# An mLSTM cell and a gated feed-forward block on one core: constant products in TensorE's pauses, late gates first, both sums of the first group at once, and weight blocks converted two columns ahead

## The chip, the cores and the metric

The kernel runs on one core of one Trainium2 chip. The metric is the device time in microseconds (us), from start to end of one execution; for the kernel before it is the median of three runs.

## The reference

Two blocks follow each other. The first is an mLSTM cell for 4 batches x 8 heads, 768 steps and a head dimension of 40. For each batch and head it keeps a matrix state and runs

```python
m_new  = maximum(f + m, i)
f_stab, i_stab = exp(f + m - m_new), exp(i - m_new)
C = f_stab * C + i_stab * outer(v_t, k_t)
n = f_stab * n + i_stab * k_t
y_t = sigmoid(o_t) * (C @ q_t) / maximum(abs(n . q_t), 1)
```

The heads of a step are then joined to a row of 320 numbers, 3072 rows in all, and the second block is `out = (silu(x @ w_gate) * (x @ w_val)) @ w_out` with 1536 hidden columns. The activations are 32-bit floats. The three weight matrices are 64-bit floats.

## The kernel before

**Groups.** The 768 steps are cut into six groups of 128 steps (L, `NG` = 6), and each group into two halves of 64 (SUB). One group of all batches makes 512 rows of x (`TW`). For each group the kernel does the cell, then the hidden layer, then the projection. The cell of group n is woven into the hidden layer of group n-1; only the cell of group 0 stands alone at the start.

**The cell of a group** is worked in two parts P (16 of the 32 batch-heads each). `turn` transposes k and q on TensorE (L292) and copies them out of PSUM. `scores` multiplies them (L307), `weigh` (L314) multiplies by the weights `w_sb`, which come from the gates. `weigh_values` (L317) scales v; `add` (L329) makes the sums of outer products of a half, for one half or for both (`parts`); `next_state` (L339 to L343) decays the old state with `dec` and adds the sum. A ring of three states `C_ring` is kept. `attend` (L351, L356) multiplies the queries by the states and the weights by v. `gather` (L366 to L377) adds both and forms the denominator, `gate` (L382) multiplies by the sigmoid of o, `divide` (L387, L389) writes x, and `seam` (L402) transposes x into `xT`.

**The gates.** The weights need running sums and running maxima of the gates. Those of group 0 (`f0`, `i0`, L258 to L265) are done first, spread over 128 partitions. The ten later halves lie in `f_sb`, `i_sb` (32 partitions x 640): `late_sums` (L270 to L274), `late_maxima` (L277 to L282, which also stores the maxima to DRAM as `M_dram`) and `late_turns` (L501 to L516: ten transposes, then the decays `dec` through one matmul). These three are run after the first, second and third hidden column of group 0. For the groups from 1 on, `weights_load` (L410) loads the maxima back in a spread form, `weights_sub` (L414), `weights_mask` (L419) and `weights_exp` (L423) make `w_sb` of them, and `sig` (L426) is the sigmoid of o.

**The hidden layer** (`hidden`, L527 to L531) does one column block m of 128 at a time, twelve in a group: ten matmuls of 512 columns for gate and value together, a SiLU on ScalarE, a product on VectorE into `h_sb`. **The projection** of group 0 (`project_all`, L548) holds four sums of 320 columns in PSUM and goes through m; the later groups' (`project`, L541) go one batch after the other. `result` (L535, L536) copies the sums out of PSUM on ScalarE and stores them.

**The weights.** A 64-bit float is taken as two 32-bit words and turned into a 32-bit float on the engines, block by block (18 blocks j: twelve hidden columns, six of w_out): `scale` on ScalarE (L180, L181; the low words are scaled in place), `join` on VectorE (L189, L190), `rounded` on GpSimd or VectorE (L197). `convert` is the three in a row. Ten loads (`piece_load`) bring the words; two use memory that is needed only later (`h_sb`, `wo_sb`), the others a pool `raw` of two buffers.

**Order.** The order of instructions on each engine is the order of the calls; nothing is moved by a scheduler. Each engine works through its list in order. `slots[m]` lists what is issued after the hidden column m of group 0, and `after[m]` what follows step m of its projection; a second `slots` does it for the later groups. In the kernel before, block m + 2 is converted after column m has been issued, its activation and product included. PSUM has two rings of four banks: "gen" for the hidden layer and the projection, "cell" for all the rest. A new tile in a ring waits for the reader of the tile four before it. Nearly all loads go through the queue of SyncE in program order.

`burn` (L432) issues matmuls of a tile of zeros whose result nobody reads; seven of them start the kernel.

Of the kernel before, what the change touches and what calls it, by code (L numbers as in the profile page):

```python
# [9 lines left out]
F32 = mybir.dt.float32  # L10
# [14 lines left out]
def kernel(  # L25
# [46 lines left out]
    def flat(t):  # L72
        return t.rearrange("p c t -> p (c t)")
# [45 lines left out]
    def gate_rows(a):  # L119
        return a.rearrange("b h s -> (b h) s")  # L120

    def spread_rows(a):
        return gate_rows(a)[:, 0:L].unsqueeze(0).to_broadcast([128 // BH, BH, L])

    nc.scalar.dma_start(out=flat(f0), in_=spread_rows(f_gate))
    nc.sync.dma_start(out=flat(i0), in_=spread_rows(i_gate))

# [47 lines left out]
    def scale(j):  # L175
        if j in blocks:
            lo, hi, dst = blocks[j]
            a, d = hi.shape[1], hi.shape[2]
            top = conv.tile([128, NKC * 128], F32, name="top", bufs=2).rearrange("p (a d) -> p a d", a=a)
            nc.scalar.mul(top, hi.bitcast(F32), 2.0 ** -112)  # L180
            nc.scalar.mul(lo.bitcast(I32), lo, 2.0 ** -29)  # L181
            blocks[j] = (lo, top.bitcast(U32), dst)
# [11 lines left out]
    def rounded(j, eng=None):  # L194
        if j in blocks:
            lo, both, dst = blocks.pop(j)
            (eng or nc.gpsimd).tensor_tensor(dst.bitcast(I32), both.bitcast(I32), lo.bitcast(I32), op=ALU.add)  # L197
# [10 lines left out]
    piece_load(0)  # L208
    load(o_sb, o_gate, 0, 0)
    load(o_sb, o_gate, 0, 1)  # L210
    nc.sync.dma_start(out=flat(f_sb), in_=gate_rows(f_gate)[:, L:])
    nc.sync.dma_start(out=flat(i_sb), in_=gate_rows(i_gate)[:, L:])
# [71 lines left out]
    M_dram = tc.dram_tile([BH, S - L], F32, name="M_dram")  # L284

# [37 lines left out]
    def add(P, parts=(0, 1)):  # L323
        ps = {i: small("add") for i in parts}
        order = QUAD if len(parts) == 2 else ((parts[0], 0), (parts[0], 1))
        for a in range(UA):
            for i, two in order:
                h = P * UH + 2 * a + two
                nc.tensor.matmul(ps[i][half(two), a, :], lhsT=k_sb[half(i), h, :], rhs=vw_sb[half(i), h, :],  # L329
                                 start=True, stop=True)  # L330
        return ps
# [4 lines left out]
    def next_state(s, P, ps):  # L336
        a = slice(P * UA, (P + 1) * UA)
        if s == 0:
            nc.scalar.copy(state(1)[:, a], ps)  # L339
            return  # L340
        nc.gpsimd.tensor_tensor(state(s + 1)[:, a], state(s)[:, a],  # L341
                                dec[:, s - 1, a].unsqueeze(2).to_broadcast([128, UA, D1]), op=ALU.mult)
        nc.vector.tensor_tensor(state(s + 1)[:, a], state(s + 1)[:, a], ps, op=ALU.add)  # L343
# [115 lines left out]
    A, V, G = nc.scalar, nc.vector, nc.gpsimd  # L459
    first_weights(0)  # L460
    turn(0, (V, V), (A, A))
    first_weights(1)
    tpe = bank("tp_e")[:, 0:BH]
    nc.tensor.transpose(tpe, flat(e0[0:BH]), idb)
    nc.vector.tensor_copy(e_T[:, 0], tpe)
    weigh_values(G, 0)
    sp = scores(0)
    weigh(0, sp)
    ps = add(0, (0,))
    next_state(0, 0, ps[0])  # L470
    turn_one(1, k_sb, kT, (A, A))
    at = attend(0, 0)
    y0, den0 = gather(0, 0, *at)
    turn_one(1, q_sb, qT, (A, V))
    weigh_values(G, 1)
    sp = scores(1)
    weigh(1, sp)
    ps = add(1, (0,))
    next_state(0, 1, ps[0])
    scale(0)  # L480
    join(0)
    at = attend(0, 1)
    sig(0)
    sig(1)
    gate(0, y0, G)
    divide(0, den0, G)
    rounded(0)
    y1, den1 = gather(0, 1, *at)
    seam(0, 0, (A, A, A, A))
    gate(1, y1, V)  # L490
    divide(1, den1)
    seam(0, 1, (A, V, A, V))
    scale(1)
    join(1)
    rounded(1, V)

    def late_turns():
        for src, dst in ((i_sb, g_T), (step1, e_T)):
            tp = bank("tp_g")[:, 0:NG * BH].rearrange("p (c h) -> p c h", h=BH)
            for c in range(1, NG):  # L500
                nc.tensor.transpose(tp[:, c, :], flat(src[:, 2 * c - 2:2 * c]), idb)  # L501
            nc.vector.tensor_copy(dst[:, 1:, :], tp[:, 1:, :])
        pair = early.tile([BH, PP], F32)
        nc.vector.reduce_sum(pair, idb.rearrange("p (a two) -> p a two", two=2), axis=AX.X)
        half_s = early.tile([BH, 2], F32)
        nc.vector.reduce_sum(half_s, idb.rearrange("p (a two) -> p two a", two=2), axis=AX.X)
        halves = early.tile([BH, 2, DP], F32)
        nc.vector.tensor_copy(halves, half_s.unsqueeze(2).to_broadcast([BH, 2, DP]))
        dec_r = early.tile([BH, NS - 1, PP], F32)
        for e, c0, n in ((e0[0:BH, 1:], 0, 1), (step1, 1, NS - 2)):  # L510
            nc.vector.tensor_tensor(dec_r[:, c0:c0 + n], pair.unsqueeze(1).to_broadcast([BH, n, PP]),
                                    e[:, :, last].to_broadcast([BH, n, PP]), op=ALU.mult)
        dps = bank("dec_ps")[:, 0:(NS - 1) * PP]
        nc.tensor.matmul(dps, lhsT=halves.rearrange("p a b -> p (a b)"), rhs=dec_r.rearrange("p c a -> p (c a)"),
                         start=True, stop=True)
        nc.vector.tensor_copy(dec.rearrange("p c a -> p (c a)"), dps)  # L516


# [3 lines left out]
    def hidden(g, m):  # L522
        ps = [bank("gv_ps", "gen") for _ in range(2)]
        x = xT(g)
        for kc in range(NKC):
            for i in range(2):
                nc.tensor.matmul(ps[i], lhsT=wgv_sb[half(i), PAIRS[kc][i], ts(m, 128)], rhs=x[half(i), kc, :],  # L527
                                 start=(kc == 0), stop=(kc == NKC - 1))
        sg = work.tile([128, TW], F32, name="sg")
        nc.scalar.activation(sg, ps[0], AF.Silu)  # L530
        nc.vector.tensor_tensor(hid(g, m), sg, ps[1], op=ALU.mult)  # L531
# [32 lines left out]
    def do_add(parts=(0, 1)):  # L564
        for P in range(2):
            live["add", P] = add(P, parts)

    def do_state(s, P):
        for i, ps in live.pop(("add", P)).items():
            next_state(s + i, P, ps)  # L570
# [15 lines left out]
    def first_state():  # L586
        do_add((1,))
        for P in range(2):
            do_state(0, P)

    def load_all(dst, a, n):
        for P in range(2):
# [4 lines left out]

    slots = {
        0: [run(convert, 2), run(late_sums)],
        1: [run(convert, 3), run(late_maxima), run(piece_load, 4), run(piece_load, 5)],  # L600
        2: [run(convert, 4), run(late_turns)],
        3: [run(convert, 5), run(first_state), run(load_all, k_sb, k, 1), run(load_all, q_sb, q, 1),
            run(weights_load, 1), run(load_all, v_sb, v, 1)],
        4: [run(convert, 6)],
        5: [run(convert, 7), run(piece_load, 6)],
        6: [run(convert, 8), run(turn, 0, (A, A), (A, V))],
        7: [run(convert, 9), run(turn, 1, (A, A), (A, V)), run(weights_sub, 1, 0), run(weights_mask, 0),
            run(piece_load, 7)],
        8: [run(convert, 10), run(weights_sub, 1, 1), run(weights_mask, 1), run(load_all, o_sb, o_gate, 1)],
        9: [run(convert, 11), run(piece_load, 8), run(weights_exp, 0), run(weights_exp, 1),  # L610
            run(weigh_values, G, 0), run(weigh_values, G, 1), run(do_scores), run(do_weigh, 0)],
        10: [run(convert, 12), run(do_weigh, 1), run(do_add), run(do_state, 2, 0), run(do_state, 2, 1)],
        11: [run(convert, 13), run(piece_load, 9), run(do_attend, 1, 0), run(do_gather, 1, 0, False)],
    }
    for m in range(NFC):
        hidden(0, m)
        for f in slots[m]:
            f()
    after = {
        0: [run(do_attend, 1, 1), run(convert, 14)],  # L620
        1: [run(do_gather, 1, 1, False), run(sig, 0), run(sig, 1), run(do_gate, 0), run(do_gate, 1),
            run(load_all, k_sb, k, 2), run(load_all, q_sb, q, 2), run(load_all, v_sb, v, 2), run(weights_load, 2)],
        2: [run(convert, 15)],
        3: [run(do_divide, 0), run(do_divide, 1), run(load_all, o_sb, o_gate, 2)],
        4: [run(convert, 16)],
        5: [run(seam, 1, 0, (A, V, A, V)), run(seam, 1, 1, (A, V, A, V))],
        6: [run(convert, 17)],
        7: [run(weights_sub, 2, 0), run(weights_mask, 0)],
        8: [run(weights_sub, 2, 1), run(weights_mask, 1)],
        9: [run(weights_exp, 0), run(weights_exp, 1)],  # L630
        10: [run(sig, 0), run(sig, 1), run(weigh_values, G, 0)],
        11: [run(weigh_values, G, 1)],
    }
    project_all(0, after)
    early_scope.close()
# [4 lines left out]
    for g in range(1, NG):  # L640
        n, f = g + 1, g + 2
        slots = {m: [] for m in range(NFC)}
        if n < NG:
# [9 lines left out]
            slots[10] = [run(do_divide, 1)]  # L653
            slots[11] = [run(seam, n, 0, (A, V, A, V)), run(seam, n, 1, (A, V, A, V))]
# [51 lines left out]
```

## Time and profile before

| what | us |
|---|---|
| time, median of 3 runs (616.28 to 620.67) | 618.82 |
| span of the profiled execution | 614.9 |
| TensorE busy | 578.1 (94%) |
| VectorE busy | 210.7 (34%) |
| ScalarE busy | 150.8 (25%) |
| GpSimd busy | 111.5 (18%) |
| mean granted TensorE clock | 0.955 |
| first hidden matmul of group 0 starts | 37.84 |
| projection of group 0 starts, ends | 127.91, 159.03 |
| hidden layer of group 1 starts | 166.64 |

Times count from the start of the span. PE is TensorE, PEld its weight loads, DVE is VectorE, ACT is ScalarE and POOL is GpSimd. L527 is line 527 of the listing above. In a line of the timeline stand the start, the time it took, the engine and line, what was written from what, and the number of instructions; in brackets stand the idle time of the engine just before and what ended it. One line can stand for several instructions of a kind. In a table by stage each engine has its busy time and (x) its number of instructions; then come the granted clock of TensorE (1.00 is full), the busy share of the DMA engines and what they moved in GB/s. The chain of work goes back from the last instruction to what released each; its lines have a start, a time and the work.

From 166 us on, each of the groups 1 to 4 takes 91.3 us (the projections of the groups begin at 233.97, 325.31, 416.64 and 507.96 us in the chain), and TensorE is nearly always busy there. Ahead of it lie the cell of group 0, the hidden layer of group 0 with the cell of group 1 and most of the conversion of the weights, and the projection of group 0.

### The profile page before, as it was taken

To read this page: it belongs to the slowest core of one execution; us is meant where nothing else is said; L and a number is where in the kernel's file an instruction comes from. 1 tells how busy PE (TensorE), PEld (TensorE's weight loads), DVE (VectorE), ACT (ScalarE), POOL (GpSimd) and SP (SyncE) were. 2 spreads that over 40 slices of the span, in tenths; PEclk is the share of its full clock that TensorE was granted. 3 is DMA by queue.
4 is the path that set the end of the run, shared out by engine and by line. 5 is a ranking of instruction groups with operands and counts; after the bars stand their busy time and mean duration, and the time that the engine had idled before them with its cause. 6 is when DMAs were issued, how large, how long until landed. Compare 5 with 4: busy or idle time off the path is not lost.

```text
span 614.9 us, 13142 instructions
## 1 busy us (share of the span) xinstructions
PE 578.1 (94%) x5880; PEld 342.6 (56%) x5880; DVE 210.7 (34%) x371; ACT 150.8 (25%) x240; POOL 111.5 (18%) x109
## 2 busy tenths in 40 slices
PE   8868699799599999999999999999999999999997
PEld 5733345466385556655556655557655557644465
DVE  4457446575123452023452023452023550011100
ACT  3434346351431011521011521111521111011100
POOL 2133135733500213200213200113200110000000
PEclk9659699799899999999999999999999999999999
DMA  9881799359330443030562020451000000000000
GB/s 125 160 168 31 151 167 229 99 120 164 67 66 1 67 90 55 22 54 2 67 103 42 33 44 6 62 111 34 33 1 4 1 3 16 28 0 1 0 12 32
DMA packets 129920, 37.92 MB, mean 62 GB/s; under 512 B 120424, under 2 KB 125032, under 8 KB 129864
## 3 DMA queue, kind: packets, MB, share of 16 engines
q1 hardware_dynamic: 129732, 37.02, 33.6%
q8 instruction: 46, 0.75, 0.6%
q14 instruction: 10, 0.08, 0.1%
q10 hardware_dynamic: 132, 0.07, 0.0%
HBM read 33.06 MB, written 4.01 MB: 60 GB/s over the span
## 4 chain that ended last, share of the span: by engine, by line
PE 72%; ACT 1%; POOL 0%; issue 0%; ACTq 0%
PE gv_ps L527 43%; PE o_ps L541 21%; PE inter L351 1%; PE sp L307 1%; PE add L329 1%; PE tp_kq L292 1%; PE intra L356 1%; PE tp_x L402 1%; ACT sg L530 0%; POOL w_sb L419 0%; ACT xT L115 0%; ACT o_sb L426 0%; ACT L426 0%; ACT w_sb L423 0%; ACT z_sb L535 0%
## 5 line engine op out<-in xcount | busy, mean ns | idle before, releaser
L527 PE MATMUL gv_ps<-xT,wgv_sb 64*128 64x512 f32 x1440 | 328.9, 606 | 11.5 <-ACT z_sb L535 7.6
L527 PEld LDWEIGHTS gv_ps<-xT,wgv_sb 64*128 64x128 f32 x1440 | 146.4, 191 | 168.8 <-issue 149.9
L531 DVE TENSOR_TENSOR h_sb<-sg,gv_ps 128x512 f32<-128x512 f32 x72 | 49.4, 687 | 325.9 <-ACT sg L530 287.8
L541 PE MATMUL o_ps<-wo_sb,h_sb 128*128 128x320 f32 x480 | 130.5, 433 | 0.0
L530 ACT ACTIVATE sg<-gv_ps 128x512 f32<-128x512 f32 x72 | 43.0, 597 | 298.1 <-PE gv_ps L527 298.1
L541 PEld LDWEIGHTS o_ps<-wo_sb,h_sb 128*128 128x128 f32 x480 | 90.8, 190 | 38.2 <-issue 0.8
L341 POOL TENSOR_TENSOR C<-C,dec 128x328 f32<-128x328 f32 x22 | 15.9, 734 | 172.5 <-DVE C L343 172.5
L535 ACT COPY z_sb<-o_ps 128x320 f32<-128x320 f32 x24 | 10.1, 424 | 106.3 <-PE o_ps L541 104.4
L419 POOL TENSOR_SCALAR_AFFINE_SELECT w_sb<-w_sb 64x1024 f32<-64x1024 f32 x20 | 26.0, 1302 | 26.8 <-DVE w_sb L414 25.9
L548 PE MATMUL o_ps<-wo_sb,h_sb 128*128 128x320 f32 x96 | 26.6, 436 | 0.0
L382 POOL TENSOR_TENSOR o_sb<-o_sb,y_sb 128x640 f32<-128x640 f32 x11 | 15.7, 1428 | 58.3 <-DVE y_sb L373 48.4
L317 POOL TENSOR_TENSOR vw_sb<-v_sb,w_sb 128x656 f32<-128x656 f32 x12 | 15.4, 1301 | 40.7 <-issue 26.6
L373 DVE TENSOR_TENSOR y_sb<-y_sb,intra 64x328 f32<-64x328 f32 x44 | 21.7, 493 | 2.5 <-PE intra L356 1.6
L548 PEld LDWEIGHTS o_ps<-wo_sb,h_sb 128*128 128x128 f32 x96 | 18.0, 190 | 7.3
L329 PEld LDWEIGHTS add<-vw_sb,k_sb 64*64 64x64 f32 x768 | 17.2, 152 | 8.7 <-issue 4.1
L329 PE MATMUL add<-vw_sb,k_sb 64*64 64x41 f32 x768 | 18.4, 244 | 3.8 <-DVE w_sb L314 3.8
L402 PE MATMUL tp_x<-ident,x_sb 64*128 64x64 f32 x240 | 14.2, 245 | 5.9 <-ACT xT L115 3.2
L351 PEld LDWEIGHTS inter<-C,qT 64*64 64x64 f32 x768 | 14.2, 149 | 7.9 <-issue 6.8
L314 DVE TENSOR_TENSOR w_sb<-sp,w_sb 128x512 f32<-128x512 f32 x24 | 15.4, 683 | 8.0 <-PE sp L307 5.0
L402 PEld LDWEIGHTS tp_x<-ident,x_sb 64*128 64x128 f32 x240 | 11.5, 150 | 11.0 <-ACT xT L115 4.4
L307 PE MATMUL sp<-qT,kT 64*64 64x64 f32 x768 | 14.3, 223 | 3.0 <-ACT qT L115 1.4
L307 PEld LDWEIGHTS sp<-qT,kT 64*64 64x64 f32 x768 | 12.7, 137 | 7.6 <-issue 4.3
(111 smaller groups left out, 371.4 us busy)
## 6 DMA issues: line engine op xcount, KB each, us to landing
w_sb<-M_dram SPq DMA_DIRECT2D x10, 512.0 KB, 7.4
k_sb<-in_k_dram SPq DMA_DIRECT2D x12, 320.0 KB, 6.0
q_sb<-in_q_dram SPq DMA_DIRECT2D x12, 320.0 KB, 6.3
v_sb<-in_v_dram SPq DMA_DIRECT2D x12, 320.0 KB, 6.5
o_sb<-in_o_gate_dram SPq DMA_DIRECT2D x12, 320.0 KB, 6.9
raw<-in_moe_w_out_dram SPq DMA_DIRECT2D x3, 1280.0 KB, 5.9
out_dram<-z_sb SPq DMA_DIRECT2D x24, 160.0 KB, 1.8
raw<-in_moe_w_gate_dram SPq DMA_DIRECT2D x3, 640.0 KB, 8.5
```

Source lines behind the costliest of these rows:

```text
L307: nc.tensor.matmul(sp[two][half(i), a, :], lhsT=kT[half(two), P * UA + a, half(i)], rhs=qT[half(two), P * UA + a, half(i)], start=True, st ...
L329: nc.tensor.matmul(ps[i][half(two), a, :], lhsT=k_sb[half(i), h, :], rhs=vw_sb[half(i), h, :], start=True, stop=True)
L341: nc.gpsimd.tensor_tensor(state(s + 1)[:, a], state(s)[:, a], dec[:, s - 1, a].unsqueeze(2).to_broadcast([128, UA, D1]), op=ALU.mult)
L351: nc.tensor.matmul(inter[two][half(i), a, :], lhsT=qT[half(two), P * UA + a, half(i)], rhs=state(2 * n + i)[half(two), P * UA + a, :], sta ...
L373: nc.vector.tensor_tensor(t, t, intra[i][half(c)], op=ALU.add)
L402: nc.tensor.transpose(tp[i][:, c - cs[0], b, :], x_sb[half(i), 2 * P + b, ds(PAIRS[c][0] * HP, 2 * HP)], ident[half(i), half(i)])
L419: nc.gpsimd.affine_select(w, w, compare_op=ALU.is_ge, fill=NEG, base=0, pattern=[[0, UH], [1, SUB]], channel_multiplier=-1)
L527: nc.tensor.matmul(ps[i], lhsT=wgv_sb[half(i), PAIRS[kc][i], ts(m, 128)], rhs=x[half(i), kc, :], start=(kc == 0), stop=(kc == NKC - 1))
L530: nc.scalar.activation(sg, ps[0], AF.Silu)
L531: nc.vector.tensor_tensor(hid(g, m), sg, ps[1], op=ALU.mult)
L541: nc.tensor.matmul(p, lhsT=hid(g, m)[:, ts(u, L)], rhs=wo_sb[:, m, :], start=(m == 0), stop=(m == NFC - 1))
L548: nc.tensor.matmul(ps[u], lhsT=hid(g, m)[:, ts(u, L)], rhs=wo_sb[:, m, :], start=(m == 0), stop=(m == NFC - 1))
```

## The change

It has five parts, all in how the work is ordered; the arithmetic stays, but for one sum that is formed another way.

1. **Constant products.** `burn` is called six more times, in places of the start where TensorE waits for other engines: 3, 2, 4, 3, 4 and 8 matmuls, 24 in all. They are to keep TensorE's clock up. Each call takes a bank of the "cell" ring.
2. **Late gates first.** `f_sb` and `i_sb` are loaded at the beginning, through ScalarE's queue; `late_sums` is issued at the start, right after group 0's gates; `late_maxima` moves from the second hidden column to the first. The decays are split: `decay_rows` after the second column, the transposes after the third, the matmul after the fourth. The first weights of columns (`piece_load(0)`) come after o.
3. **Both sums of the first group at once.** `first_sums` forms the sums of both halves in the start and copies them to states 1 and 2; `second_state` later adds the decayed state 1 to state 2 (two operations on GpSimd). The separate second sums after the fourth column go.
4. **Two columns ahead.** The conversion of block m + 2 is issued inside `hidden(0, m)`, ahead of its activation and product. The scaled low words get a tile of their own (`low`), and `top` and `low` have one buffer each, where `top` had two. The blocks 9, 10 and 11 are rounded on VectorE.
5. **Order elsewhere.** gate and divide of group 0 go to VectorE, and the first `weigh_values` too. The slots of the cell of group 1 move by up to a column; exponentials, sigmoids and `weigh_values` of group 2 follow the projection of group 0 and its output copies, instead of standing ahead of them; in the later groups `seam(n, 0)` moves from slot 11 to slot 10.

```diff
+    nc.scalar.dma_start(out=flat(f_sb), in_=gate_rows(f_gate)[:, L:])
+    nc.scalar.dma_start(out=flat(i_sb), in_=gate_rows(i_gate)[:, L:])
...
-            top = conv.tile([128, NKC * 128], F32, name="top", bufs=2).rearrange("p (a d) -> p a d", a=a)
+            top = conv.tile([128, NKC * 128], F32, name="top", bufs=1).rearrange("p (a d) -> p a d", a=a)
             nc.scalar.mul(top, hi.bitcast(F32), 2.0 ** -112)
-            nc.scalar.mul(lo.bitcast(I32), lo, 2.0 ** -29)
+            low = conv.tile([128, NKC * 128], I32, name="low", bufs=1).rearrange("p (a d) -> p a d", a=a)
+            nc.scalar.mul(low, lo, 2.0 ** -29)
...
-    piece_load(0)
     load(o_sb, o_gate, 0, 0)
     load(o_sb, o_gate, 0, 1)
-    nc.sync.dma_start(out=flat(f_sb), in_=gate_rows(f_gate)[:, L:])
-    nc.sync.dma_start(out=flat(i_sb), in_=gate_rows(i_gate)[:, L:])
+    piece_load(0)
     piece_load(1)
...
     M_dram = tc.dram_tile([BH, S - L], F32, name="M_dram")
+    late_sums()
...
+    def first_sums(P):
+        ps = add(P)
+        for i in range(2):
+            nc.scalar.copy(state(i + 1)[:, P * UA:(P + 1) * UA], ps[i])
+
     first_weights(0)
     turn(0, (V, V), (A, A))
     first_weights(1)
+    burn(3)
+    weigh_values(V, 0)
+    sp = scores(0)
+    weigh(0, sp)
+    first_sums(0)
+    turn_one(1, k_sb, kT, (A, A))
     tpe = bank("tp_e")[:, 0:BH]
...
-    weigh_values(G, 0)
-    sp = scores(0)
-    weigh(0, sp)
-    ps = add(0, (0,))
-    next_state(0, 0, ps[0])
-    turn_one(1, k_sb, kT, (A, A))
+    burn(2)
     at = attend(0, 0)
+    weigh_values(G, 1)
     y0, den0 = gather(0, 0, *at)
     turn_one(1, q_sb, qT, (A, V))
-    weigh_values(G, 1)
+    burn(4)
+    sig(0)
+    sig(1)
     sp = scores(1)
     weigh(1, sp)
-    ps = add(1, (0,))
-    next_state(0, 1, ps[0])
+    first_sums(1)
+    burn(3)
+    gate(0, y0, V)
+    divide(0, den0)
+    at = attend(0, 1)
+    y1, den1 = gather(0, 1, *at)
     scale(0)
-    join(0)
-    at = attend(0, 1)
-    sig(0)
-    sig(1)
-    gate(0, y0, G)
-    divide(0, den0, G)
-    rounded(0)
-    y1, den1 = gather(0, 1, *at)
+    burn(4)
     seam(0, 0, (A, A, A, A))
+    burn(8)
     gate(1, y1, V)
     divide(1, den1)
+    join(0)
+    rounded(0, V)
+    scale(1)
     seam(0, 1, (A, V, A, V))
-    scale(1)
     join(1)
-    rounded(1, V)
+    rounded(1)
...
+    def second_state():
+        old = work.tile([128, PP, D1], F32, name="y_sb")
+        nc.gpsimd.tensor_tensor(old, state(1), dec[:, 0].unsqueeze(2).to_broadcast([128, PP, D1]), op=ALU.mult)
+        nc.gpsimd.tensor_tensor(state(2), state(2), old, op=ALU.add)
...
-    def hidden(g, m):
+    def hidden(g, m, first=()):
...
+        for f in first:
+            f()
         sg = work.tile([128, TW], F32, name="sg")
...
+    on_vector = (9, 10, 11)
     slots = {
...
+        0: [run(load_all, k_sb, k, 1), run(load_all, q_sb, q, 1), run(piece_load, 5), run(late_maxima)],
+        1: [run(decay_rows)],
+        2: [run(late_turns), run(weights_load, 1)],
+        3: [run(decay)],
+        4: [run(second_state), run(piece_load, 6), run(load_all, v_sb, v, 1)],
+        5: [run(turn, 0, (A, A), (A, V))],
+        6: [run(turn, 1, (A, A), (A, V)), run(piece_load, 7)],
+        7: [run(weights_sub, 1, 0), run(weights_mask, 0)],
+        8: [run(weights_sub, 1, 1), run(weights_mask, 1), run(weights_exp, 0), run(weights_exp, 1),
+            run(weigh_values, G, 0), run(weigh_values, G, 1), run(piece_load, 8)],
+        9: [run(do_scores), run(do_weigh, 0), run(load_all, o_sb, o_gate, 1)],
+        10: [run(do_weigh, 1), run(do_add), run(do_state, 2, 0), run(do_state, 2, 1), run(piece_load, 9)],
+        11: [run(do_attend, 1, 0), run(do_gather, 1, 0, False)],
     }
+    piece_load(4)
     for m in range(NFC):
-        hidden(0, m)
+        hidden(0, m, [run(convert, m + 2, V if m + 2 in on_vector else None)])
...
     project_all(0, after)
+    weights_exp(0)
+    weights_exp(1)
+    sig(0)
+    sig(1)
+    weigh_values(G, 0)
+    weigh_values(G, 1)
...
-            slots[10] = [run(do_divide, 1)]
-            slots[11] = [run(seam, n, 0, (A, V, A, V)), run(seam, n, 1, (A, V, A, V))]
+            slots[10] = [run(do_divide, 1), run(seam, n, 0, (A, V, A, V))]
+            slots[11] = [run(seam, n, 1, (A, V, A, V))]
```

## The prediction

> **What bounds the kernel now.** TensorE, but not evenly. I read the page's slices first, then the table by stage, then TensorE's timeline with its idle times, last the chain of work.
>
> ```profile
> PE   8868699799599999999999999999999999999997
> PEclk9659699799899999999999999999999999999999
> ```
>
> Each slice is 15.4 us. From the twelfth on TensorE is busy at full clock; the loss lies in the first eleven.
>
> ```profile
> core 0: us, PE busy (x) PEld busy (x) DVE busy (x) ACT busy (x) POOL busy (x), PEclk, DMA share, GB/s
> 0.00:37.80 37.80, 29.21 (x708) 22.60 (x708) 19.82 (x48) 15.35 (x30) 10.93 (x20) 0.72 0.96 155
> 37.80:58.30 20.50, 18.49 (x61) 7.26 (x62) 11.47 (x16) 7.78 (x10) 4.99 (x3) 0.77 0.28 54
> 58.30:67.90 9.60, 1.94 (x12) 1.33 (x12) 5.83 (x13) 3.95 (x5) 2.42 (x2) 0.64 0.92 188
> 104.50:127.90 23.40, 18.56 (x426) 11.91 (x424) 13.01 (x19) 10.64 (x14) 13.21 (x11) 0.85 0.40 98
> 127.90:166.60 38.70, 30.58 (x269) 21.68 (x264) 20.73 (x37) 16.11 (x23) 20.28 (x16) 0.96 0.79 130
> ```
>
> No stage is full on any other engine. The clock column shows a second loss: a slower TensorE in the first 68 us.
>
> ```profile
> 37.84 2.04 PE L527 MATMUL gv_ps<-xT,wgv_sb 64*128 64x512 f32 x2 [0.69 <-ACT xT L115]
> 41.28 11.87 PE L527 MATMUL gv_ps<-xT,wgv_sb 64*128 64x512 f32 x38 [1.40 <-DVE wgv_sb L197]
> 60.93 0.67 PE L501 MATMUL tp_g<-ident,keep 32*128 32x32 f32 x5 [2.21 <-ACT keep L281]
> 67.04 0.95 PE L514 MATMUL dec_ps<-dec_r,halves 32*128 32x176 f32 x2 [5.45 <-DVE dec_r L511]
> ...
> 114.55 0.31 PE L329 MATMUL add<-vw_sb,k_sb 64*64 64x41 f32 x2 [2.27 <-DVE w_sb L314]
> 120.16 5.70 PE L527 MATMUL gv_ps<-xT,wgv_sb 64*128 64x512 f32 x20
> ```
>
> In brackets stands the idle time before, and its releaser. The gates' scans and decays (L270 to L516) hold TensorE for 2.21 and 5.45 us in the third column.
>
> ```profile
> 160.16 1.14 POOL w_sb L419
> 161.37 1.15 POOL w_sb L419
> 162.54 1.06 ACT w_sb L423
> 164.91 1.36 ACT o_sb L426 x2
> 166.27 0.32 ACT z_sb L535
> ...
> 322.82 0.58 ACT sg L530
> 323.40 0.49 ACT xT L115
> ```
>
> The chain: after group 0's projection ends at 159.03, mask, exponential and sigmoid of group 2 stand ahead of the output copies on ScalarE, and TensorE idles 7.61 us. The last two lines recur four times (231, 323, 414, 505 us): a seam waits for its copies.
>
> **What the skill says.** "TensorE: Matmul & The Clock Gate", What's actually happening: windows of about 3.4 us; too idle a one halves the clock, a busy one restores it. The trace agrees: 20 matmuls of a column take 4.32 us at full clock (8.64 for 40 in the chain), the first 40 products took 13.9, and the clock returned at 47.4 after products without a gap from 41.28. "SBUF — State Buffer", Who interferes with whom: a VectorE operation with two SBUF inputs and a GpSimd one that reads SBUF lock each other out. The trace agrees: `weights_sub` took 2.28 us where a rounding on GpSimd had begun before it, and 1.22 where it came first (the rounding then took 2.33 instead of 1.56). "DMA: Bandwidth & Descriptors", Issuing engines are not separate DMA queues: an issue from ScalarE saves sequencer time, not bandwidth; so 160 KB of late gates ahead of k and q cost about 1 us at the 155 GB/s of the first stage. "ScalarE: Activation LUTs", What ACT_TABLE_LOAD costs: 1.28 us, plus a drain; the trace has the 1.28, with the next instruction directly behind (163.62, then 164.91). I use 1.28.
>
> **Part by part.**
>
> *Start, to the first gated product (37.84 us before).* Late gates first: scan 1.47, subtraction about 0.8 (like L280, 0.81, free of GpSimd), two copies 0.3, together 2.6 us on VectorE. They fit the 3.05 us it idled before the first kT copy at 9.42, if the gates land by 7 us. Bounds 0 and 3 (a landing 5.9 us after issue, as f_sb had); I take 0, and 1 for the data behind them. Both sums at once: 32 matmuls instead of 16, but on four quadrants. A whole group's sums take 2.01 us at full clock, so 1.0 for one half, against 1.91 for the 16 on one row half at half clock. `burn`: 24 constant products. A full-clock one takes 0.22 us (4.32/20), a half-clock one 0.45 (3.17/7 in the first seven), so 5.2 to 10.8 us. Three lie beside qT copies (1.1), two beside kT copies (1.1), four beside the den chain and qT, three beside the state copies, four beside gather(0,1). Eight before seam(0,1) stand beside gate and divide, and overhang by 1 us at full clock, 3 at half. Tracing the queues: first values on VectorE, scores(0) to 13.7; scores(1) 21.3 to 22.3; attend(0,1) to 26.1 (30.15 before); gather, gate(1), divide(1) to 29.9; burns and seam(0,1) to 32.2; join and rounding of block 0 until 31.7 ahead of VectorE's copies. ScalarE's `scale(1)` is queued ahead of its seam copies and with one buffer waits for that rounding: 0.8, then copies 0.75. First product 33.3 at full clock; with some work at half, **34.5: gain 3.3**, bounds 4.5 and 0.
>
> *Columns of group 0 (37.84 to 127.91 = 90.1 us before).* Floor of TensorE's work after: 12 x 4.32 = 51.8; turns 2.0, scores 2.0, sums 2.0, attend(1,0) 2.1; late turns and decay 1.6: 61.5. The 2.06 us of second sums (L329 at 74.07) leave. Added back:
> - The clock starts at half: one window, 1.7 (0 to 5).
> - `late_maxima` after column 0: about 3.4 on VectorE, 0.73 on ScalarE, then scale(3), a table load 1.28 and the gate of column 1 with its product 1.3. Column 3 needs block 3 and those banks: 1.2 late (0 to 3).
> - Two columns ahead: a block now needs scale 1.5, join 1.3, rounding 1.56 to 2.67, some 5 us, within two columns (8.6) rather than one. With one `top`, `low` and `both`, blocks follow at join plus rounding, 2.9 to 4.0, under 4.32. So L197's waits go: 0.4 is left.
> - Slots 8 to 10: mask(1) waits for a subtraction queued behind a join and ends some 6 us after column 8; exp(1) 1.06, scale(11) 1.5, table load 1.28 and the gate 0.6 end at 10 to 11; product, weigh(0) 1.29, join 1.3, product, weigh(1) 1.29 free the sums' banks at 15 to 16, where TensorE came to the sums at 10.7. It loses 3.6 of idle and some 1.6 of clock: 5.2 (3 to 9). Before, this place cost about 8.
>
> Sum 61.5 + 1.7 + 1.2 + 0.4 + 5.2 = 70.0: **gain 20.1**. `second_state`, 2.6 us on GpSimd in slot 4, lies in the two columns' lead.
>
> *Projection of group 0 (127.91 to 159.03).* 48 matmuls are 26.05, attend and seam the rest. Blocks 14 to 17 and the gather keep their places: 0.
>
> *Its end.* The output copies (0.42 each) now precede the exponentials: TensorE resumes after 0.8. But ScalarE then does the other two copies with a wait for the store (2), exponentials and sigmoids with three table loads (2.1 + 1.4 + 3.8), ending some 10.6 us after the projection; column 2's banks and the second turn wait: 2.5. So 3.3 for 7.61 idle plus 2.1 of half clock (6.40 for 4.32): **gain 6.4** (3 to 8).
>
> *Later groups.* seam(n,0) one slot earlier: its copies lie beside column 11, and the 1.07 of the chain's last two lines leaves, four times: **gain 4** (2 to 4.4).
>
> Sum 3.3 + 20.1 + 6.4 + 4 = 33.8: 618.8 - 33.8 = **585 us**.
>
> **Rivals.** (a) *Half the gain: the clock does not hold and the single buffers convoy.* Against: 40 products without a gap restored it. For: 95% busy with small matmuls from 26.5 to 30.15 did not. Half clock over three more windows in the columns 5, the start without gain 3.3, slots 8 to 10 as long as before 3, the group's end 3: 14 back, 599 us. (b) *No change: another engine takes the place.* ScalarE gets the copies, gates and scales in one order, and each `low` waits for GpSimd. At 5.5 us a column (scale, join, slow rounding in series), 12 x 1.2 = 14; with (a)'s 14 and seams unmoved (4), 617. Against: VectorE 13.0, ScalarE 10.6, GpSimd 13.2 of 23.4 us in the worst stage; they have room. (c) *Slower.* Late gates hold VectorE 3, every burn falls on the path at half clock 10.8, convoy 14, end stall kept 6.4, seams 4: 38 against 33.8, 623 us. For: all queues are in order. Against: the burns stand where TensorE waits anyway. (d) *Better:* no loss in slots 8 to 10, full clock throughout: 577.
>
> **Numbers.** Forecast 585 with 0.58, (a) 0.24, (b) 0.06, (c) 0.06, (d) 0.06. The range runs from (d) a little lower, for the bounds at their good end, to (a) with 4 us more: 574 to 603. Faster by over 1% means below 612.6: 0.88 from forecast, (a) and (d). Same 0.06, slower 0.06.
>
> **What would show it.** First product near 34 to 35 us; the gates' two waits gone from the third and fourth columns; projection of group 0 from about 105 to 136; a wait of the sums for VectorE near 95 us; no wait over 2 us for the output copy; tp_x waits after 230 us gone. The forecast is wrong if VectorE waits for a gate DMA before kT, if burns stand in the chain, or if products wait for roundings in every column.

## The result, and the profile after

| | before | after |
|---|---|---|
| time, median of 4 runs | 618.38 us (616.28 to 620.67) | 589.44 us (588.58 to 590.76) |
| ratio | | 0.9533, 95% interval 0.9494 to 0.9573 |
| span of the profiled execution | 614.9 us | 587.2 us |
| first hidden matmul of group 0 | 37.84 us | 45.58 us |
| projection of group 0 starts | 127.91 us | 113.82 us |
| hidden layer of group 1 starts | 166.64 us | 143.99 us |
| mean granted TensorE clock | 0.955 | 0.991 |

The change brings 28.9 us; 33.8 were forecast. First the profile's slices of the kernel after (14.7 us each), and the line of its DMA queues that will matter later (packets, MB, share of the time).

```profile
PE   7759998999999999999999999999999999999997
...
PEclk9879999999999999999999999999999999999999
...
q8 instruction: 46, 0.75, 0.6%
```

TensorE is now nearly full from the fourth slice on, where it was from the twelfth; the first three are no better than before. The table by stage has the columns that were explained for the kernel before.

```profile
0.00:45.60 45.60, 30.78 (x798) 20.31 (x798) 23.75 (x58) 17.42 (x33) 5.36 (x16) 0.89 0.99 167
45.60:59.40 13.80, 13.80 (x72) 6.41 (x72) 7.80 (x15) 9.87 (x13) 4.62 (x3) 1.00 1.36 147
59.40:94.90 35.50, 34.31 (x207) 16.03 (x206) 22.00 (x33) 18.45 (x29) 15.88 (x12) 1.00 0.78 160
94.90:113.80 18.90, 16.68 (x425) 10.16 (x424) 12.11 (x20) 9.35 (x13) 8.36 (x8) 1.00 0.66 176
113.80:144.00 30.20, 30.20 (x274) 21.27 (x266) 20.85 (x35) 9.77 (x16) 16.24 (x12) 1.00 0.93 126
```

From 45.6 us on the clock is full in every stage, and the projection (last row) has no idle time. But the start has 14.8 us in which TensorE does nothing. Its timeline says what ended these times:

```profile
10.69 0.71 PE L294 MATMUL tp_kq<-ident,q_sb 64*128 64x64 f32 x16 [1.11 <-DMA q_sb<-in_q_dram]
...
18.15 0.96 PE L349 MATMUL inter<-C,qT 64*64 64x41 f32 x51 [0.77 <-issue]
...
22.47 0.40 PE L294 MATMUL tp_kq<-ident,q_sb 64*128 64x64 f32 x6 [1.78 <-issue]
...
28.47 0.43 PE L330 MATMUL add<-vw_sb,k_sb 64*64 64x41 f32 x11 [1.36 <-issue]
...
30.54 0.93 PE L354 MATMUL intra<-v_sb,w_sb 64*64 64x41 f32 x49
37.85 0.66 PE L354 MATMUL intra<-v_sb,w_sb 64*64 64x41 f32 x15 [6.38 <-issue]
...
45.58 13.15 PE L546 MATMUL gv_ps<-xT,wgv_sb 64*128 64x512 f32 x60 [0.99 <-ACT xT L115]
```

"issue" means that TensorE waited for nothing that the profile shows. The 6.38 us fall in the middle of attend(0,1), between two matmuls of the same kind and line. The four such pauses sum to 10.3 us. The last line is the good side of it: the first three columns, 60 records, take 13.15 us at full clock; before, the first 40 took 13.9.

Later in group 0, three waits for roundings (L200) and two for products of the weights (L316) are left; then, in group 1, three short ones for copies:

```profile
79.38 5.37 PE L546 MATMUL gv_ps<-xT,wgv_sb 64*128 64x512 f32 x22
84.93 4.56 PE L546 MATMUL gv_ps<-xT,wgv_sb 64*128 64x512 f32 x20 [0.19 <-DVE wgv_sb L200]
90.50 4.56 PE L546 MATMUL gv_ps<-xT,wgv_sb 64*128 64x512 f32 x18 [1.00 <-DVE wgv_sb L200]
94.98 2.09 PE L309 MATMUL sp<-qT,kT 64*64 64x64 f32 x128
97.01 1.12 PE L546 MATMUL gv_ps<-xT,wgv_sb 64*128 64x512 f32 x2
99.56 4.56 PE L546 MATMUL gv_ps<-xT,wgv_sb 64*128 64x512 f32 x18 [1.43 <-DVE wgv_sb L200]
104.05 1.14 PE L330 MATMUL add<-vw_sb,k_sb 64*64 64x41 f32 x64
105.66 0.28 PE L330 MATMUL add<-vw_sb,k_sb 64*64 64x41 f32 x2 [0.47 <-DVE w_sb L316]
106.26 1.14 PE L330 MATMUL add<-vw_sb,k_sb 64*64 64x41 f32 x62 [0.32 <-DVE w_sb L316]
...
154.26 0.27 PE L294 MATMUL tp_kq<-ident,k_sb 64*128 64x64 f32 x1 [0.38 <-ACT kT L115]
154.75 0.70 PE L294 MATMUL tp_kq<-ident,k_sb 64*128 64x64 f32 x15 [0.22 <-ACT qT L115]
...
155.71 0.71 PE L294 MATMUL tp_kq<-ident,q_sb 64*128 64x64 f32 x15 [0.25 <-DVE qT L117]
```

The idle times in brackets understate what the roundings cost. From start to start, the columns 7 to 9 take 15.60 us (79.38 to 94.98) and column 10 takes 7.04 (97.01 to 104.05); in the kernel of experiment 9 below, which has no such waits, columns 7 to 9 take 13.03. By this measure the three waits, 2.6 us of idle, cost some 5 us: the first two records of column 10 ran ahead (97.01), and the other 18 still took 4.56 us, as long as a whole column of 20.

Where the 27.7 us between the two spans lie, by these start times and those of group 1's projection (233.97 and 209.65):

| stage | before | after | gain | forecast |
|---|---|---|---|---|
| start | 37.84 | 45.58 | -7.7 | 3.3 |
| columns of group 0 | 90.07 | 68.24 | 21.8 | 20.1 |
| projection of group 0 and its end | 38.73 | 30.17 | 8.6 | |
| hidden layer of group 1 | 67.33 | 65.66 | 1.7 | 6.4 with the row above, and 1 of the seams' 4 |
| the rest | 380.93 | 377.55 | 3.4 | 3 |

One term of the sum is wrong by 11 us, and has the wrong sign.

### The profile page after: what moved, and what is told of

Its sections match the earlier page's. It is cut to its first block, busy times and chain, and to the rows that moved or that the text cites. A ratio compares the mean times of both kernels' runs of the same rounds, so it can differ in the third digit from the quotient of the medians.

```text
span 587.2 us, 13173 instructions
## 1 busy us (share of the span) xinstructions
PE 564.7 (96%) x5904; PEld 326.2 (56%) x5904; DVE 210.0 (36%) x376; ACT 152.0 (26%) x242; POOL 101.9 (17%) x102
## 4 chain that ended last, share of the span: by engine, by line
PE 80%; ACT 1%; DVE 1%; DMA 0%; issue 0%; ACTq 0%; DVEq 0%
PE gv_ps L546 45%; PE o_ps L562 22%; PE o_ps L569 4%; PE inter L349 2%; PE intra L354 2%; PE add L330 2%; PE sp L309 1%; PE tp_kq L294 1%; PE tp_x L400 1%; ACT w_sb L421 0%; DMA out_dram<-z_sb 0%; ACT o_sb L424 0%; ACT L551 0%; ACT L424 0%; ACT L421 0%
## 5 line engine op out<-in xcount | busy, mean ns | idle before, releaser
L546 PE MATMUL gv_ps<-xT,wgv_sb 64*128 64x512 f32 x1440 | 321.7, 594 | 3.6 <-DVE wgv_sb L200 2.6
L546 PEld LDWEIGHTS gv_ps<-xT,wgv_sb 64*128 64x128 f32 x1440 | 138.1, 187 | 158.5 <-issue 151.2
L380 POOL TENSOR_TENSOR o_sb<-o_sb,y_sb 128x640 f32<-128x640 f32 x10 | 14.2, 1426 | 48.3 <-DVE y_sb L371 48.3
L354 PE MATMUL intra<-v_sb,w_sb 64*64 64x41 f32 x768 | 14.5, 229 | 6.4 <-issue 6.4
L349 PEld LDWEIGHTS inter<-C,qT 64*64 64x64 f32 x768 | 12.5, 134 | 9.0 <-issue 7.8
L330 PEld LDWEIGHTS add<-vw_sb,k_sb 64*64 64x64 f32 x768 | 13.2, 141 | 6.9 <-issue 5.7
L354 PEld LDWEIGHTS intra<-v_sb,w_sb 64*64 64x64 f32 x768 | 13.3, 136 | 6.4 <-issue 6.4
L330 PE MATMUL add<-vw_sb,k_sb 64*64 64x41 f32 x768 | 14.2, 233 | 2.7 <-issue 1.4
L316 DVE TENSOR_TENSOR w_sb<-sp,w_sb 128x512 f32<-128x512 f32 x24 | 15.4, 683 | 2.3 <-PE sp L309 2.2
L200 POOL TENSOR_TENSOR wgv_sb<-both,low 128x640 int32<-128x640 int32 x8 | 12.3, 1542 | 21.3 <-DVE both L193 21.3
L193 DVE SCALAR_TENSOR_TENSOR both<-top,both 128x640 uint32<-128x640 uint32 x18 | 15.7, 870 | 0.6
```

The costliest lines, as they stand in the source:

```text
L193: nc.vector.scalar_tensor_tensor(both, in0=top, scalar=0x80000000, in1=both, op0=ALU.bitwise_and, op1=ALU.bitwise_or)
L316: nc.vector.tensor_tensor(w2[:, two], sp[two], w2[:, two], op=ALU.mult)
L349: nc.tensor.matmul(inter[two][half(i), a, :], lhsT=qT[half(two), P * UA + a, half(i)], rhs=state(2 * n + i)[half(two), P * UA + a, :], sta ...
L354: nc.tensor.matmul(intra[i][half(c), a, :], lhsT=w_sb[half(i), h, :], rhs=v_sb[half(i), h, :], start=True, stop=True)
```

## The experiments

**What stops TensorE in the start.** If one counts the records of TensorE between the ends of the pauses, there are 6 + 4 + 64 + 53 = 127 from 22.47 to 28.47, and 11 + 3 + 64 + 49 = 127 from 28.47 to 37.85. A record is a matmul with its load of weights, two instructions; so the pauses come every 256 instructions or so (a record may be missing). The profile gives 46 packets of the kind "instruction" with 0.75 MB on queue q8, 16 KB each; TensorE's 5904 matmuls and 5904 loads of weights are 46 times 256. The trace's packets of this queue:

```
kernel after: starts   lasts    TensorE goes on    goes on after landing
              19.80    1.23     22.47              1.44
              25.38    1.33     28.47              1.76
              34.93    1.29     37.85              1.63
```

Every pause ends 1.4 to 1.8 us after such a packet has landed (the first too: landed at 16.66, on at 18.15). The Trainium skill, "Runtime: NRT & Kernel Launch", Instruction fetch mechanics, says that an engine's instructions come in blocks of 16 KiB, 256 instructions, over a DMA queue of its own, and that the cost of a block's edge is mostly hidden. Size and spacing agree with this trace. Hidden it is not: 6.5 us lie between TensorE's start on a block (28.47) and the start of the next packet (34.93). The theory, then: the block stands behind the weights, which SyncE issued from 19 to 26 us without a break. Two rivals: TensorE uses up instructions faster than they can come, whatever else is loaded; or the constant products make the pauses.

*1. The large weight loads held back.*

```diff
     load(o_sb, o_gate, 0, 1)
     piece_load(0)
     piece_load(1)
-    piece_load(2, h_sb[:, NH - NKC:])
-    piece_load(3, wo_sb)
...
     gate(0, y0, V)
     divide(0, den0)
+    nc.vector.memset(h_sb[:, NH - NKC, 0:2], 0.0)
+    piece_load(2, h_sb[:, NH - NKC:])
+    piece_load(3, wo_sb)
     at = attend(0, 1)
```

> The changed kernel, with the two large weight loads (pieces 2 and 3, 2.56 MB) held behind divide(0) by a small memset of their buffer on VectorE. Theory: the 6.4 us in which TensorE waits for nothing in attend(0,1) are a wait for its next block of 256 instructions, which comes over the same DMA engines and stands behind these loads. Then that pause falls under 1.5 us, the first hidden product starts at 38 to 40 us instead of 45.6, and the time is 582 to 585 us. Rival: TensorE simply uses up instructions faster than they can be fetched, whatever else is loaded; then the pause stays near 6 us and the time near 589. Third way: the held weights now come too late, and hidden columns 2 to 4 wait for roundings by more than 2 us.

The time was 586.03 us, ratio 0.9478 (0.9442 to 0.9513). TensorE's timeline of this kernel:

```profile
21.91 0.40 PE L292 MATMUL tp_kq<-ident,q_sb 64*128 64x64 f32 x6 [1.78 <-issue]
...
27.90 0.43 PE L328 MATMUL add<-vw_sb,k_sb 64*64 64x41 f32 x11 [1.45 <-issue]
...
31.80 0.44 PE L352 MATMUL intra<-v_sb,w_sb 64*64 64x41 f32 x15 [0.90 <-issue]
...
39.31 13.14 PE L547 MATMUL gv_ps<-xT,wgv_sb 64*128 64x512 f32 x60 [1.47 <-ACT xT L115]
```

The pause falls at the same place, with 49 matmuls before and 15 after it, and is 0.90 instead of 6.38 us. The packet starts 1.2 us after TensorE began the block before (27.90, then 29.06). The next one, with the held loads under way (issued from 28.13 us on), again starts 7.0 us after (31.80, then 38.75), but there TensorE doesn't reach the end of its block so soon. The two pauses ahead of the hold stay at 1.78 and 1.45, as they should: nothing was changed for them. The first product comes at 39.31, 6.3 us earlier. That the loads hold up the block is shown; whether in the DMA engines or in memory, no run separates. That TensorE is simply too fast accounts at most for what is left. No early column waits for a held weight. The time gained 3.4 us in the medians, a little short of the 4 to 7 expected, and the two intervals still overlap: in this profile the columns took 71.0 us instead of 68.2, with 1.7 of the difference in one column that is partly at half clock (18 records from 94.28 in 6.25 us, 4.56 in the kernel after) and 1.0 in the wait of column 9.

*2. Without the constant products.* All six calls of `burn` with 3, 2, 4, 3, 4 and 8 are taken out.

```diff
-    burn(3)
...
-    burn(8)
```

> The changed kernel without the 24 added constant products (the seven at the very start stay). Theory of the fetch: the pauses of TensorE stay and only move by 24 instruction pairs; the first hidden product starts at 44 to 47 us, at half clock for one or two windows; time 588 to 594 us. Rival: the constant products themselves, or the PSUM banks they take, make the pauses; then the first product starts before 37 us and the time is below 582.

590.46 us, ratio 0.9565 (0.9533 to 0.9598).

```profile
37.76 0.44 PE L354 MATMUL intra<-v_sb,w_sb 64*64 64x41 f32 x3 [6.18 <-issue]
...
45.22 15.20 PE L540 MATMUL gv_ps<-xT,wgv_sb 64*128 64x512 f32 x60 [2.06 <-ACT xT L115]
```

The pause stays (6.18), 12 records later in the same operation, after the 12 constant products that preceded it are gone. So they do not make it. The first three columns take 15.20 instead of 13.15: the warm clock is worth 2.1 us there, and the start is 0.4 longer with them. In the whole the difference, 1.0 us, is within the intervals. The same was tried on top of the held loads (*11* below).

*3. The kernel before, with the gates' loads alone moved.* In the kernel before, SyncE issued the gates' loads from 21.31 to 24.35 us and the large weights only from 24.39, and a packet of instructions started at 24.60.

```diff
     nc.sync.dma_start(out=flat(i0), in_=spread_rows(i_gate))
+    nc.scalar.dma_start(out=flat(f_sb), in_=gate_rows(f_gate)[:, L:])
+    nc.scalar.dma_start(out=flat(i_sb), in_=gate_rows(i_gate)[:, L:])
...
-    nc.sync.dma_start(out=flat(f_sb), in_=gate_rows(f_gate)[:, L:])
-    nc.sync.dma_start(out=flat(i_sb), in_=gate_rows(i_gate)[:, L:])
```

> The kernel before, with only the two loads of the late gates moved to ScalarE's queue at the start (late_sums stays after the first column). In the kernel before, SyncE's queue stood still for some 3 us at 24 us, and a block of instructions came just then. Theory of the fetch: without the two loads in SyncE's list the weights follow at once, the block meets full DMA engines, a pause of 2 to 7 us comes up in attend(0,1), and the time rises to 620 to 625 us. Rival: no such pause; the weights come earlier and the time is 615 to 618.

619.3 us, ratio 1.002 (1.0002 to 1.0039), between the two expectations. The pause I expected did not come:

```profile
27.84 0.31 PE L351 MATMUL inter<-C,qT 64*64 64x41 f32 x3 [0.46 <-issue]
...
37.60 2.04 PE L527 MATMUL gv_ps<-xT,wgv_sb 64*128 64x512 f32 x2 [0.69 <-ACT xT L115]
```

A miss, and an instructive one. The packet of 25.31 was late by only 0.46. The next one started at 34.47, 6.6 us after TensorE began a block at 27.84, just as late as in the kernel after (6.5). But the block that it brought was not needed before the first column: from 27.84 there are only 3 + 64 + 40 matmuls to the first product, 107 of some 128. The kernel before has 708 records of TensorE ahead of its first product, the one after 796: 24 constant products and 64 records of second sums more. The slow fetch is in this kernel as in the changed one; in the changed one a block's edge lies inside the attend that everything waits for.

**What the other parts are worth.**

*4. The seams alone, in the kernel before.*

```diff
-            slots[10] = [run(do_divide, 1)]
-            slots[11] = [run(seam, n, 0, (A, V, A, V)), run(seam, n, 1, (A, V, A, V))]
+            slots[10] = [run(do_divide, 1), run(seam, n, 0, (A, V, A, V))]
+            slots[11] = [run(seam, n, 1, (A, V, A, V))]
```

> The kernel before, with only seam(n,0) of the later groups moved from slot 11 to slot 10. If the four waits of the seams for their copies leave and nothing takes their place: 4.0 to 5.0 us less, 613 to 614.5. If the first seam now waits for VectorE's copies queued behind divide(1): no change.

611.74 us, ratio 0.9896 (0.9861 to 0.993), which is 4.3 to 8.6 us less; the median lies below the expected 613 to 614.5, the interval reaches into it. In the chain of work both seams now stand without a wait:

```profile
317.81 0.61 PE tp_x L402 x20
318.42 4.35 PE gv_ps L527 x20
322.77 0.62 PE tp_x L402 x20
323.39 6.66 PE o_ps L541 x24
```

From one projection's start to the next (233.25 to 323.39) are 90.14 us, against 91.34. The projection of group 4 begins at 503.62 in this profile's chain, against 507.96: 4.3 us.

*5. The end of group 0's projection alone, in the kernel before.*

```diff
-        9: [run(weights_exp, 0), run(weights_exp, 1)],
-        10: [run(sig, 0), run(sig, 1), run(weigh_values, G, 0)],
-        11: [run(weigh_values, G, 1)],
     }
     project_all(0, after)
+    weights_exp(0)
+    weights_exp(1)
+    sig(0)
+    sig(1)
+    weigh_values(G, 0)
+    weigh_values(G, 1)
```

> The kernel before, with only the end of group 0's projection in the new order: exponentials, sigmoids and weigh_values of group 2 after the output copies. Theory: the 7.6 us of idle and the half clock after it (2.1) leave, and some 0.9 us of waits for ScalarE's copies come in: 8 to 9.5 us less, 609 to 610.5. Rival: the wait only moves to the third column of group 1, whose banks wait for the gate behind the exponentials: under 4 us less.

608.9 us, ratio 0.9856 (0.9822 to 0.9891), 6.7 to 11.0 us less; the expected 8 to 9.5 lie inside. TensorE's timeline:

```profile
158.59 4.56 PE L527 MATMUL gv_ps<-xT,wgv_sb 64*128 64x512 f32 x20
...
168.84 0.27 PE L292 MATMUL tp_kq<-ident,k_sb 64*128 64x64 f32 x1 [0.34 <-ACT kT L115]
```

No idle time ahead of group 1's first column, full clock, and 0.8 us of waits for copies in the turn that follows (0.34 + 0.22 + 0.24): what the chain of the kernel before showed to be lost is won almost whole.

*6. The gates' work back in its old places, in the kernel after.*

```diff
-    late_sums()
...
-        0: [..., run(late_maxima)],
-        1: [run(decay_rows)],
-        2: [run(late_turns), run(weights_load, 1)],
-        3: [run(decay)],
+        0: [..., run(late_sums)],
+        1: [run(late_maxima)],
+        2: [run(late_turns), run(decay_rows), run(decay), run(weights_load, 1)],
+        3: [],
```

> The changed kernel with late_sums, late_maxima and the decay work back in their old places after columns 0, 1 and 2 (their loads stay at the start). Theory: TensorE waits again for the exponential and for dec_r in the third column, 5 to 8 us, with the clock falling after it: 595 to 600 us. Rival: two columns ahead already hide most of it: under 592.

597.54 us, ratio 0.9661 (0.9636 to 0.9685), 8.1 more than the kernel after.

```profile
61.01 0.49 PE L513 MATMUL tp_g<-ident,keep 32*128 32x32 f32 x5 [1.41 <-ACT keep L282]
66.20 0.95 PE L527 MATMUL dec_ps<-dec_r,halves 32*128 32x176 f32 x2 [4.70 <-DVE dec_r L522]
```

Both waits of the kernel before are back, 6.1 us together. Most of the rest is clock: the 60 records of hidden columns behind them, from 67.08 us on, take 14.96 us, where the first 60 of the kernel after took 13.15. The start is not shorter without the gates' work in it (first product at 46.02, against 45.58).

*7. Conversion one column ahead, in the kernel after.*

```diff
-        hidden(0, m, [run(convert, m + 2, V if m + 2 in on_vector else None)])
+        hidden(0, m)
+        convert(m + 2, V if m + 2 in on_vector else None)
```

> The changed kernel with the conversion of block m + 2 issued after column m's activation and product, as before; all else stays. My prediction's theory: the block's chain of some 5 us no longer fits beside one column of 4.32, so products wait for roundings in most columns and slots 8 to 10 get longer: 3 to 8 us more, 592.5 to 597.5. Rival: the kernel before lost only 3.3 us to roundings in all, so the conversion ahead is worth little once the gates are out of the way: at most 1 us more.

604.06 us, ratio 0.9757 (0.9714 to 0.9799): 14.6 more, beyond both expectations. TensorE's waits in the first 160 us, summed up (total, times, longest):

```profile
PE gv_ps L546 <- DVE wgv_sb L200: 8.0, 3, 3.1
...
PE gv_ps L546 <- POOL wgv_sb L200: 3.4, 2, 2.1
```

8.0 of the waits are for the three roundings on VectorE. By start times this profile's columns 7 to 10 lose 7.1 us more than those of the kernel after. VectorE's own timeline in the kernel after shows what is peculiar about these:

```profile
84.06 0.82 DVE L200 CUSTOM_DVE_ANT_0 wgv_sb<-both,low 128x1280 uint16<-128x1280 uint16 x1 [1.27 <-PE gv_ps L546]
```

The rounding of block 9 waits for TensorE's column 7, and column 8 (84.93 above) for the rounding, though it doesn't use that block. The trace's list of instructions agrees on the first: the roundings of the blocks 9 to 11 on VectorE wait for TensorE's semaphore, those of the other columns' blocks on GpSimd do not. So a rounding that could lie beside a column stands between two of them. Why this form has the waits is not shown.

*8. One column ahead, all roundings on GpSimd.*

```diff
-    on_vector = (9, 10, 11)
+    on_vector = ()
```

(on the kernel of 7)

> The changed kernel with the conversion one column ahead, and all roundings on GpSimd. One column ahead cost 14.6 us, but 8 us of its waits were for roundings on VectorE, which start only when the column before has ended. Theory: that combination, not the distance alone, made most of it; then this one takes 593 to 598 us, some 4 to 8 more than the changed kernel. Rival: the distance alone costs as much: 601 or more.

596.34 us, ratio 0.963 (0.9595 to 0.9665), 6.9 more than the kernel after.

```profile
PE gv_ps L546 <- POOL wgv_sb L200: 4.5, 3, 2.1
...
PE add L330 <- DVE w_sb L316: 3.6, 4, 2.6
```

So 7.7 of run 7's loss came with VectorE's roundings. The rest, 6.9, is the cost of the shorter distance, with 4.5 of waits of products for roundings; as the move to GpSimd may itself gain some 2 us (9), the distance alone may cost up to 9. The changed kernel with all roundings on GpSimd was not run.

*9. All roundings on GpSimd, with the held loads.* The same edit on the kernel of 1.

> The kernel with held weight loads, with the blocks 9, 10 and 11 rounded on GpSimd like the others. In the trace the rounding on VectorE starts only when the matmuls of the column before have ended, and the next column waits for it: 0.2, 1.0 and 1.4 us. Theory: these waits leave, 583 to 584 us. Rival: GpSimd is full with masks and value products just there, the roundings come late instead: 586 or more.

584.06 us, ratio 0.9445 (0.9422 to 0.9467), against 586.03 without it: between both expectations, and the intervals overlap. The waits for roundings are gone (TensorE's waits have no line for them), but the sums wait in their place:

```profile
95.90 0.31 PE L328 MATMUL add<-vw_sb,k_sb 64*64 64x41 f32 x2 [2.09 <-DVE w_sb L314]
...
99.04 0.40 PE L328 MATMUL add<-vw_sb,k_sb 64*64 64x41 f32 x2 [1.41 <-DVE w_sb L314]
99.64 1.94 PE L328 MATMUL add<-vw_sb,k_sb 64*64 64x41 f32 x62 [0.20 <-DVE w_sb L314]
101.51 6.01 PE L547 MATMUL gv_ps<-xT,wgv_sb 64*128 64x512 f32 x20
```

4.0 us of idle and then half clock (1.94 for a second half of sums that takes 1.14, 6.01 for a column of 4.56 in these records). This is the stall that the prediction had put into slots 8 to 10. In sum the twelve columns take 69.07 us (40.39 to 109.46) instead of 71.01.

*10. Masks a column earlier, on the kernel of 9.*

```diff
-        6: [run(turn, 1, (A, A), (A, V)), run(piece_load, 7)],
-        7: [run(weights_sub, 1, 0), run(weights_mask, 0)],
-        8: [run(weights_sub, 1, 1), run(weights_mask, 1), run(weights_exp, 0), run(weights_exp, 1),
+        6: [run(turn, 1, (A, A), (A, V)), run(piece_load, 7), run(weights_sub, 1, 0), run(weights_mask, 0)],
+        7: [run(weights_sub, 1, 1), run(weights_mask, 1)],
+        8: [run(weights_exp, 0), run(weights_exp, 1),
```

> The kernel with held weight loads and all roundings on GpSimd, with subtraction and mask of group 1's weights one column earlier (slots 6 and 7), the exponentials staying in slot 8. Theory: what is left in the tenth and eleventh columns (4 us of waits of the sums for the products, then some 2.5 us at half clock) comes from mask(1) ending some 6 us after column 8 and holding the exponential, the scaling and the gate behind it on ScalarE. With the masks done before, 4 to 6 us leave: 578 to 580.5. Rival: VectorE's chain of products and joins alone keeps the sums' banks: under 1.5 us less.

579.77 us (578.93 to 580.63), ratio 0.9364 (0.9329 to 0.94): 4.3 less than 9, within the expectation.

```profile
95.57 0.28 PE L328 MATMUL add<-vw_sb,k_sb 64*64 64x41 f32 x2 [1.02 <-DVE w_sb L314]
96.17 1.49 PE L328 MATMUL add<-vw_sb,k_sb 64*64 64x41 f32 x62 [0.32 <-DVE w_sb L314]
97.59 5.83 PE L547 MATMUL gv_ps<-xT,wgv_sb 64*128 64x512 f32 x20
```

Idle 1.3 instead of 4.0; one half-clock window is left. This version is 9.7 us faster than the changed kernel and some 39 faster than the one before.

*11. Held loads without constant products.* The edit of 2 on the kernel of 1.

> The kernel with held weight loads, without the 24 added constant products. Theory: they only warm the clock, so without them part of the start and the first hidden column run at half clock: 1 to 3 us more than with them, 587 to 589. Rival: they stand in the path and fill instruction blocks; without them the start is shorter: 583 to 585.

586.38 us, ratio 0.948 (0.9437 to 0.9523), against 586.03 with them: no difference that these runs can tell. The first product starts at 38.32, 1.0 earlier than with them; its three columns take 15.80 us, 2.7 more. So at the end of the third column this profile is 1.7 us behind (54.12 against 52.45); later columns make that good, as the half-clock column that the profile of 1 had does not show in it.

## Why the prediction was right, and where it was wrong

The time lies in the range and near the forecast; the reasons hold for the later stages in the main, and the term of the start failed. That the sum still came within 5 us is in part luck. By the two spans, the start brought 11.0 less than forecast, the columns 1.7 more, and all behind them 3.3 more.

- **Start: wrong.** The step "attend(0,1) to 26.1" traced queues, transfers and PSUM banks, and had no term for TensorE's own instructions. scores(0) ended at 13.68 as traced (13.7). From there on the four pauses add 10.3 us; 45.58 less these is 35.3, near the 34.5 forecast. Experiment 1 took 5.5 us of the longest away by moving loads alone. Experiment 2 rules out the constant products as its cause; but they and the second sums move a block's edge into the path (3).
- **Late gates: right.** They cost VectorE a wait of 0.95 us for the transfer and put its first kT copy at 9.82 instead of 9.42, with no wait of TensorE for it; q came 1.1 us later, where 1 us was estimated. Both waits in the third column went, and come back if the work is put back, which makes the start no shorter (6).
- **Both sums at once: right.** 64 records of add took 1.14 us, 1.0 estimated, and the 2.06 us of second sums left the columns. No run takes this part back alone.
- **Constant products: half right.** The price was right (four in 1.04 us at 22.80, eight in 1.89 at 41.93), and the first column ran at full clock, where I had added 1.7. But with and without them the times agree within the intervals, in the changed kernel (2) and with held loads (11).
- **Columns: right in size (21.8 for 20.1), partly for other reasons.** No half-clock window at the start and no delay by `late_maxima`: 2.9 us that I had added did not come. For slots 8 to 10 I had 3.6 of idle from the sums' wait plus 1.6 of clock; measured were 0.8 for the sums, some 5 by start times for the roundings on VectorE, and no loss of clock. That the two terms are alike is luck. The prediction had not seen that these roundings wait for the column. They were hiding the other stall: with them on GpSimd (9) the sums wait 4.0 us and the clock falls, as reckoned, and the cause named, the late mask, is confirmed by 10.
- **Two columns ahead: right for the blocks on GpSimd.** No product waits for one of their roundings, so the single buffers did not convoy the blocks; the distance is worth some 7 to 9 us (8). For the blocks on VectorE 0.4 was left in the forecast, and some 5 came.
- **End of the projection: mis-sized low.** 3.3 us were left over in the forecast, 0.85 in the trace (0.38 + 0.22 + 0.25). In the trace the first copy starts at 142.48, before the last matmul ends at 144.06, and ScalarE is through with the exponentials, sigmoids and table loads at 153.12, 9.1 us after the projection, where I had put 10.6. With the projection itself 0.9 us shorter and about 1 us of the seam in group 1, the two rows of the table give 10.3 for 6.4.
- **Later groups: right.** 3.4 and a part of group 1's 1.7, for 4; alone, the seams brought 4.3 in a profile (4).

## What to carry to other kernels

Large loads can hold up an engine's own instructions, as they did here: where an engine goes through many small instructions while large loads are queued, look for pauses that wait for nothing, count the instructions between them, and hold the loads that are not needed yet. A stall that goes may have hidden another one, and idle time can understate what a wait costs; after each edit read the same stretch again rather than the sum. And operations moved to another engine can carry other waits: look at what each form waits for.

## What the runs showed of the hardware that was not expected

- Pauses of TensorE of 0.8 to 6.4 us every 256 instructions, each ended 1.4 to 1.8 us after a packet of 16,384 bytes had landed; before the longest pause (6.38) the packet began 6.5 us after TensorE had begun the block before it, while the weights were loaded, and 1.2 us after it with these loads held.
- A copy of 32x128 on VectorE took 1.10 us in the kernel before and 0.21 in the one after; only in the former GpSimd was at work on a rounding (65.03 to 66.59) when it started (65.57).
- The clock was at 0.50 from 24 to 27 us in the kernel after, with TensorE busy all the time with small matmuls, and at full for three columns after the eight constant products at 41.93.
